# A gated state-space scan with a squared-ReLU FFN on one NeuronCore: units five to twelve put one token on each partition

## The chip, the cores and the metric

The kernel runs on one core of a Trainium2 chip. Its time is the device time of one execution in microseconds (us), given as the median of several runs; smaller is better. A profile is one execution taken by the hardware profiler, with its own span, which is a little shorter than the time of a run.

The engines are named as in the profile: PE is the matrix engine (PEld its weight loads), DVE, ACT and POOL the three elementwise engines, SP the engine that here only issues DMAs. Each engine works its own instructions off in program order. 16 DMA engines move the data.

## What is computed

Four sequences of 768 tokens, eight heads of width 32, a state of 16 x 32 per head. Per head and chunk, with `cum` the running sum of log a:

```
L   = exp(cum[i] - cum[j])  for i >= j, else 0
M   = (C @ B^T) * L                                  # scores, masked
y   = M @ x  +  (C @ state) * exp(cum)               # within the chunk, and from before
state = exp(sum) * state + sum_j B_j x_j exp(cum_last - cum_j)
...
h   = max(y_all_heads @ w_in, 0)                      # 256 -> 2048
out = (h * h) @ w_out                                 # 2048 -> 256
```

The result is a float32 array of 3072 x 256.

## The kernel before

The 3072 tokens are cut into 12 units of 256: unit k is sequence b = k mod 4, third j = k // 4 (`UNITS`). Each unit is two blocks of 128 tokens (i = 0, 1). A token's 256 = 8 x 32 values of y stand on two groups g of 128 partitions (four heads each).

**Token layout.** Each unit's B, C and x are loaded by one DMA each, with two neighbouring tokens on every partition (`ph_load`): partition p holds tokens 2p and 2p + 1, called r = 0, 1. So block i is the partitions 64i to 64i + 63 with both r. A run of the source is two tokens of one head: 128 bytes for B and C, 256 bytes for x, eight runs (heads) to each partition. The output goes out the same way, 2 KB per partition.

**Steps of one unit.** `pc`, `pb` and `px` (POOL) scale C, copy B, and scale x into `jt` and `xs`. `tr` turns `jt` into `bct`: for units 0 to 3 by PE and a copy, from unit 4 on by a DMA transpose that SP issues (`dma_tr`). `ph_mt` makes the scores of the unit from `bct` into PSUM banks 0 to 3; `ph_mask` (DVE, marks `mk`) multiplies them by the causal mask into `mts`. `ph_u` makes the new state's sum from `jt` and `xs`, `ph_carry` the part of y from the state before, `ph_intra` the part within the block. `ph_t` (ACT) copies y into `T`; then eight steps a0 to a7 (`mm1`, letters a to l for units 0 to 11) and A0 to A7 (`mm2`) are the FFN: PE, ACT's relu into `hb`, DVE's square into `h2`, PE again.

**Small products.** They use parts of the 128 x 128 array, four heads q at a time on 32 rows or columns. With two tokens per partition, `ph_mt` needs 16 matmuls (32 rows x 64 columns of weights, 256 columns streamed), `ph_intra` 32 (64 x 32, 128 streamed) and `ph_u` 16 (64 x 32, 64 streamed; 8 where j = 2, since the last state is not needed). `ph_carry` has four full-size ones.

**Order.** The whole program stands in the string `ORDER`: each mark is one step, and each engine's queue gets its instructions in that order. `rg5`, say, is `region(y=4, u=5, mt=5)`: carry of unit 4, `ph_u` of 5, intra of 4, scores of 5, then the copies. In between stand the FFN steps. `ldN` issues the three loads of unit N on SP, `trN` its transpose; the stores of a finished unit are SP's as well. The loads of units 4 to 7 are issued one behind the other early (`ld4 ... ld5 ... tr4 ... ld6 ld7`), those of units 8 to 11 one per region. Before it issues, each DMA waits for the one eight DMAs ahead of it, since the semaphores go round in eight.

Of the kernel before, what the change touches and what calls it, by code (L numbers as in the profile page):

```python
# [11 lines left out]
BF16 = mybir.dt.bfloat16  # L12
AF = mybir.ActivationFunctionType
ALU = mybir.AluOpType
# [16 lines left out]
def kernel(  # L31
# [13 lines left out]
    nc = tc.nc  # L45
    NH, S, D, N = 8, 768, 32, 16
# [8 lines left out]
        qb0 A1 b5 b4 qb1 qb2 qb5 tc2:1:v qb4 tc2:0:a a5 B0 b6 B1 a7 qa5 iv:16:32 px2 a6 mt2 B3 A2 sc2 u2 b7 us2 pb3:a  # L55
# [28 lines left out]

    UNITS = [(b, j) for j in range(3) for b in range(4)]

    eye_f = const.tile([128, 128], FP32, name="eye_f")
    eye_b = const.tile([128, 128], BF16, name="eye_b")
    mask = const.tile([128, 512], BF16, name="mask")
    tri = const.tile([128, 2, 128], BF16, name="tri")  # L90
    warm = const.tile([128, 2], BF16, name="warm")
    quad = const.tile([128, 4], FP32, name="quad")
# [24 lines left out]
    loaded = {}  # L117

    def ph_load(k, what, eng=None, hs=(0, 8)):
        b, j = UNITS[k]  # L120
        src, w = {"B": (B, N), "C": (C, N), "x": (x, D)}[what]
        t = loaded.setdefault(k, {})
        if what not in t:
            t[what] = nat.tile([128, NH, 2 * w], FP32, tag=f"{what}_nat", name=f"{what}_nat{k}")
        (eng or nc.sync).dma_start(
            out=t[what][:, hs[0]:hs[1]],
            in_=_dap(src, ((b * NH + hs[0]) * S + j * 256) * w, [[2 * w, 128], [S * w, hs[1] - hs[0]], [1, 2 * w]]))
# [24 lines left out]
    def prep_c(k, eng, P=None, gs=(0, 1)):  # L152
        b, j = UNITS[k]
        for g in gs:
            p = P_sb if P is None else P
            st = 96 if P is None else 32
            col = (j * 32 if P is None else 0) + b * 8 + 4 * g
            eng.tensor_tensor(  # L158
                out=_fap(jt[k % 3], 128 + 144 * g, [[384, 2], [32, 4], [1, 16]]),
                in0=_fap(loaded[k]["C"], 128 * g, [[16, 2], [32, 4], [1, 16]]),  # L160
                in1=_fap(p, col, [[st, 2], [1, 4], [0, 16]]), op=ALU.mult)

    def prep_b(k, eng, gs=(0, 1)):
        for g in gs:
            o = _fap(jt[k % 3], 16 * g, [[384, 2], [32, 4], [1, 16]])
            i = _fap(loaded[k]["B"], 128 * g, [[16, 2], [32, 4], [1, 16]])
            if eng is nc.scalar:
                eng.copy(out=o, in_=i)
            else:
                eng.tensor_copy(out=o, in_=i)  # L170

    def prep_x(k, eng):
        b, j = UNITS[k]
        xs = prep.tile([128, 2, 256], BF16, tag="xs", name=f"xs{k}")
        n = 2 if k >= 4 else 1
        for r in range(n):
            eng.tensor_tensor(  # L177
                out=_fap(xs, 256 * r, [[256, 2 // n], [32, 8], [1, 32]]),
                in0=_fap(loaded[k]["x"], 32 * r, [[32, 2 // n], [64, 8], [1, 32]]),
                in1=_fap(Pinv, j * 32 + b * 8 + 96 * r, [[96, 2 // n], [1, 8], [0, 32]]), op=ALU.mult)  # L180
        live.setdefault(k, {})["xs"] = xs

# [29 lines left out]
    T = {}  # L212

    def ph_mt(k):
        v = live[k]
        bct = v["bct"]
        for r in range(2):
            for u in range(2):
                for q in range(4):
                    nc.tensor.matmul(  # L220
                        pp[64 * u:64 * u + 64, q, r * 256:r * 256 + 256],
                        bct[32 * q:32 * q + 32, r, 0, u * 64:u * 64 + 64],
                        _fap(bct[32 * q:32 * q + 32], 128 + u * 64, [[128, 2], [384, 2], [1, 64]]),
                        start=True, stop=True, skip_group_check=True,
                        tile_position=(32 * q, 64 * u))
        v["mts"] = big.tile([128, 4, 2, 2, 128], BF16, tag="mts", name=f"mts{k}")

    def ph_mask(k, q):
        nc.vector.tensor_tensor(out=live[k]["mts"][:, q].rearrange("p r g i -> p (r g i)"),  # L229
                                in0=pp[:, q, :], in1=mask, op=ALU.mult)  # L230

    def ph_score(k, q):
        sc = big.tile([128, 512], BF16, tag="sc", name=f"sc{k}_{q}")
# [14 lines left out]
    def ph_carry(k, h, begun):  # L248
        for i in range(2):
            S_i = live[k]["S"][i]  # L250
            if S_i is None:
                continue
            for g in range(2):
                mm(begun, i, range(4), pp[:, h[i], g * 128:(g + 1) * 128], S_i[:, g * 128:(g + 1) * 128],
                   _fap(live[k]["bct"], 128 + g * 128 + i * 64, [[384, 2], [1, 64]]), None)
# [12 lines left out]
    def ph_intra(k, h, begun, qs=range(4)):  # L268
        v = live[k]
        for g in range(2):  # L270
            for r in range(2):
                for i in range(2):
                    for q in qs:
                        hd = 4 * g + q
                        mm(begun, i, [q], pp[32 * q:32 * q + 32, h[i], g * 128:(g + 1) * 128],
                           v["xs"][64 * i:64 * i + 64, r, hd * 32:hd * 32 + 32],
                           v["mts"][64 * i:64 * i + 64, q, r, g, :], (64 * i, 32 * q))

    def ph_t(k, h, engs=None):
        T[k] = tpool.tile([128, 2, 2, 2, 64], BF16, tag="T", name=f"T{k}")  # L280
        if engs is None and h[1] == h[0] + 1:
# [152 lines left out]
    def ph_out(blk):  # L434
        b, j = UNITS[blk]
        osb = opool.tile([128, 512], FP32, tag="osb", name=f"osb{blk}")
        nc.scalar.copy(out=osb, in_=pp[:, 6 if blk == 1 else 7, :])  # L437
        nc.sync.dma_start(out=_dap(out, (b * S + j * 256) * 256, [[512, 128], [1, 512]]), in_=osb)

    def select(t, pattern, base, mult, op=ALU.is_ge):  # L440
# [2 lines left out]
    def prep_p(n, ncol, h):  # L443

        m = n // 2

        def eye_of(n, u):
            return eye_f[0:64, u * 32:u * 32 + 32] if n == 64 else _fap(eye_f, 32 * u, [[64, 2], [1, 32]])

        for r in range(2):  # L450
            for u in range(2):
                nc.tensor.matmul(pp[64 * u:64 * u + 64, h, r * m:(r + 1) * m], _fap(cp[ncol], r, [[2, 64]]),  # L452
                                 eye_of(n, u), start=(r == 0), stop=True, skip_group_check=True,
                                 tile_position=(0, 64 * u))

    with tc.manual_schedule():
# [198 lines left out]
        def one(t):  # L655
# [12 lines left out]
            if name[0] == "q" and len(name) == 2 and name[1] in "abcdefghijkl":  # L668
# [17 lines left out]
                "mb": causal, "pk": picked, "sk": lambda: scan(0), "sp": first_p, "sn": second_scan,  # L686
# [33 lines left out]
        def store(r, eng, c0=0, n=256):  # L720
            t = opool.tile([128, n], FP32, tag="osb", name=f"osl{r}_{c0}")
            eng(out=t, in_=acc(last, r) if n == 256 else pp[:, 1 + c0 // 128, 0:n])  # L722
            (A if c0 else SQ).dma_start(out=_dap(out, (b * S + j * 256) * 256 + r * 256 + c0, [[512, 128], [1, n]]), in_=t)

        for f in range(4, 7):
            mm2(last, f, (0,))
# [37 lines left out]
```

## Time and profile before

| | |
|---|---|
| time, median of 3 runs | 117.67 us (116.44 to 117.77) |
| profiled execution: span | 115.1 us |
| PE busy | 108.9 us, 1623 matmuls |
| DVE, ACT, POOL busy | 84.2, 76.7, 49.8 us |
| moved by DMA | 13.46 MB in 47814 packets |

In the profile a line such as "L220" is the line of the kernel as printed above. In a timeline each row has the start in us from the span's start, the length, the engine (SPq is SP's queue of DMA issues), the line, the operation, what it writes and reads, how many were merged, and in brackets how long the engine stood idle before it and for whom. In the table by windows the columns are the window, its length, the busy time of PE, PEld, DVE, ACT and POOL with the number of instructions, the clock granted to PE, the mean busy share of the 16 DMA engines (over 1 where packets overlap), and GB/s.

### The profile page before, as it was taken

What the parts mean: (1) busy time and instruction counts of PE and PEld (TensorE: products, weight loads), DVE (VectorE), ACT (ScalarE), POOL (GpSimd) and SP (SyncE); (2) the same over time, 40 slices, a digit from 0 to 9 for tenths busy, and PEclk for the clock granted to TensorE, in tenths of its full rate; (3) what the DMA queues carried; (4) which work ended last, traced back from release to release, by engine and by line L of the source; (5) the groups of instructions that cost most, each with busy time, mean ns of one, the idle gap of its engine ahead of it and who ended that gap; (6) DMA issues with size and microseconds to landing.
All of it is one profiled execution on the core that took longest, in us unless ns stands there. A gap on an engine that the chain in (4) does not pass through costs nothing.

```text
span 115.1 us, 3998 instructions
## 1 busy us (share of the span) xinstructions
PE 108.9 (95%) x1623; PEld 93.5 (81%) x1623; DVE 84.2 (73%) x187; ACT 76.7 (67%) x161; POOL 49.8 (43%) x102
## 2 busy tenths in 40 slices
PE   7977969999999999999999999999999999999990
PEld 2344749978898989989989989989989899899980
DVE  2469996779599969969965989849668488445530
ACT  0655667865598756787486686786777776876840
POOL 7369972068599457548602669038020020000000
PEclk9999999999999999999999999999999999999999
DMA  1999999989999913935915926623023020020202
GB/s 29 199 196 145 199 203 189 215 167 210 180 191 211 214 24 108 160 89 155 179 46 122 178 97 123 132 95 73 0 100 68 0 100 0 6 91 0 91 0 91
DMA packets 47814, 13.46 MB, mean 117 GB/s; under 512 B 44276, under 2 KB 45876, under 8 KB 47796
## 3 DMA queue, kind: packets, MB, share of 16 engines
q1 hardware_dynamic: 43828, 10.64, 44.8%
q0 software_dynamic: 1664, 2.10, 10.8%
q10 hardware_dynamic: 2304, 0.48, 2.0%
q8 instruction: 12, 0.20, 0.8%
q14 instruction: 6, 0.05, 0.1%
HBM read 10.58 MB, written 3.15 MB: 119 GB/s over the span
## 4 chain that ended last, share of the span: by engine, by line
PE 87%; DMA 6%; POOL 2%; issue 1%; DVE 1%; ACT 1%; ACTq 0%; DVEq 0%
PE pp L430 36%; PE pp L403 36%; PE pp L245 6%; DMA w_out_b<-in_moe_w_out_dram 6%; PE pp L476 4%; PE pp L220 3%; POOL mts L238 1%; PE pp L195 1%; POOL jt L158 1%; PE pp L452 1%; DVE jt L158 0%; DVE Sd L343 0%; ACT bct L208 0%; PE pp L521 0%; ACT osl L722 0%
## 5 line engine op out<-in xcount | busy, mean ns | idle before, releaser
L408 ACT ACTIVATE hb<-pp 128x512 bf16<-128x512 f32 x96 | 55.0, 599 | 24.7 <-PE pp L403 23.1
L430 PE MATMUL pp<-w_out_b,h 128*128 128x256 bf16 (+1 forms) x400 | 54.3, 268 | 0.8 <-DMA w_out_b<-in_moe_w_out_dram 0.8
L414 DVE TENSOR_TENSOR h<-hb 128x512 bf16<-128x512 bf16 x96 | 45.0, 486 | 12.7 <-ACT hb L408 12.3
L403 PE MATMUL pp<-T,w_in_b 128*128 128x256 bf16 x384 | 54.2, 273 | 0.0
L403 PEld LDWEIGHTS <-w_in_b 128*128 128x128 bf16 x384 | 41.4, 114 | 2.2 <-issue 1.0
L430 PEld LDWEIGHTS <-h 128*128 128x128 bf16 x400 | 37.6, 98 | 5.4 <-DVE T L210 1.1
L229 DVE TENSOR_TENSOR mts<-pp,mask 128x512 bf16<-128x512 f32 x45 | 29.6, 677 | 3.3 <-PE pp L220 3.3
L331 POOL TENSOR_TENSOR Sd<-z,Pquad 128x256 bf16<-128x256 f32 x16 | 11.1, 693 | 32.9 <-DVE z L315 25.7
L177 POOL TENSOR_TENSOR xs<-x_nat,Pinv 128x256 bf16<-128x256 f32 (+1 forms) x19 | 14.4, 776 | 5.2 <-DVE Pinv L546 4.6
L158 POOL TENSOR_TENSOR jt<-C_nat,P_sb 128x128 bf16<-128x128 f32 x22 | 9.4, 449 | 1.5 <-ACT P_sb L688 1.0
L476 PE MATMUL pp<-const-bfloat16-1.0 128*128 128x512 bf16 (+2 forms) x19 | 7.3, 516 | 0.8 <-PEq L748 0.8
L315 DVE SCALAR_TENSOR_TENSOR z<-z,Ptot,us 128x64 f32<-128x64 f32 x8 | 2.2, 281 | 6.3 <-ACT us L299 5.4
L437 ACT COPY osb<-pp 128x512 f32<-128x512 f32 x11 | 6.3, 584 | 0.4 <-PE pp L430 0.4
L245 PE MATMUL pp<-mts,xs 64*32 64x128 bf16 x384 | 5.9, 219 | 0.1
L170 POOL CAST jt<-B_nat 128x128 bf16<-128x128 f32 x17 | 5.4, 341 | 1.4 <-DMA B_nat<-in_B_dram 1.4
L220 PE MATMUL pp<-bct 32*64 32x256 bf16 x192 | 5.1, 279 | 0.9 <-DVE bct L210 0.6
L476 PEld LDWEIGHTS <-const-bfloat16-1.0 128*128 128x128 bf16 x19 | 2.2, 122 | 4.0 <-issue 3.7
L245 PEld LDWEIGHTS <-xs 64*32 64x32 bf16 x384 | 4.2, 90 | 0.6 <-issue 0.4
L282 ACT CAST T<-pp 128x512 bf16<-128x512 f32 x7 | 4.1, 592 | 0.4 <-PE pp L245 0.2
L208 ACT CAST T<-pp 128x256 bf16<-128x256 f32 x8 | 2.6, 375 | 2.6 <-PE pp L245 2.6
L245 PE MATMUL pp<-bct,Sd 128*128 128x128 bf16 x40 | 4.2, 220 | 0.0
L220 PEld LDWEIGHTS <-bct 32*64 32x64 bf16 x192 | 2.1, 102 | 2.0 <-issue 0.6
(62 smaller groups left out, 53.4 us busy)
## 6 DMA issues: line engine op xcount, KB each, us to landing
x_nat<-in_x_dram SPq DMA_DIRECT2D x11, 256.0 KB, 3.7
out_dram<-osb SPq DMA_DIRECT2D x11, 256.0 KB, 3.2
B_nat<-in_B_dram SPq DMA_DIRECT2D x11, 128.0 KB, 3.1
C_nat<-in_C_dram SPq DMA_DIRECT2D x11, 128.0 KB, 3.4
w_in_b<-in_moe_w_in_dram POOLq DMA_DIRECT2D x4, 256.0 KB, 6.8
w_out_b<-in_moe_w_out_dram POOLq DMA_DIRECT2D x4, 256.0 KB, 8.2
x_nat<-in_x_dram ACTq DMA_DIRECT2D x2, 128.0 KB, 3.4
bct<-jt SPq DMA_TRANSPOSE x8, 3.6
```

The lines of the kernel that those rows point to most:

```text
L158: eng.tensor_tensor(out=_fap(jt[k % 3], 128 + 144 * g, [[384, 2], [32, 4], [1, 16]]), in0=_fap(loaded[k]["C"], 128 * g, [[16, 2], [32, 4], ...
L177: eng.tensor_tensor(out=_fap(xs, 256 * r, [[256, 2 // n], [32, 8], [1, 32]]), in0=_fap(loaded[k]["x"], 32 * r, [[32, 2 // n], [64, 8], [1, ...
L220: nc.tensor.matmul(pp[64 * u:64 * u + 64, q, r * 256:r * 256 + 256], bct[32 * q:32 * q + 32, r, 0, u * 64:u * 64 + 64], _fap(bct[32 * q:32 ...
L229: nc.vector.tensor_tensor(out=live[k]["mts"][:, q].rearrange("p r g i -> p (r g i)"), in0=pp[:, q, :], in1=mask, op=ALU.mult)
L245: nc.tensor.matmul(dst, w, v, start=bool(need), stop=False, skip_group_check=True, **({} if pos is None else {"tile_position": pos}))
L331: nc.gpsimd.tensor_tensor(out=_fap(S_d, 0, [[128, 2], [32, 4], [1, 32]]), in0=_fap(z, 0, [[32, 2], [0, 4], [1, 32]]), in1=_fap(Pquad, 4 * ...
L403: nc.tensor.matmul(pp[:, h, i * 256:(i + 1) * 256], _fap(w, g * w.shape[2] + (o // 2) * 512 + 2 * (o % 2) + i, [[4, 128]]), T[blk][:, g].r ...
L408: nc.scalar.activation(out=hb.rearrange("p i t -> p (i t)"), in_=pp[:, h, :], func=AF.Relu)
L414: nc.vector.tensor_tensor(out=h2, in0=hb, in1=hb, op=ALU.mult)
L430: nc.tensor.matmul(dst, h2[:, i, r * 128:(r + 1) * 128], w_out_b[gi][:, 2 * o + i, c0:c1], start=first, stop=(fp == 7 and i == 1), skip_gr ...
L437: nc.scalar.copy(out=osb, in_=pp[:, 6 if blk == 1 else 7, :])
L476: nc.tensor.matmul(pp[:, h, 0:int(cols)], ones_b[:, 0:128], ones_b[:, 0:int(cols)] if dep is None else dep, start=True, stop=True, skip_gr ...
```

## The change

From unit 4 on (`wide(k)`: j > 0) a partition holds one token, and block i is a whole column of 128 partitions:

- each load is issued as two DMAs, one per block, of 128 x 8 runs of one token (64 bytes for B and C, 128 bytes for x); the number of runs per unit doubles, the bytes stay;
- `prep_c`, `prep_b` and `prep_x` read the new places, with the same number of elements and instructions;
- scores: 8 matmuls of 32 x 128 weights with 256 columns in place of 16; intra: 16 of 128 x 32 in place of 32; `ph_u`: 8 (4 where j = 2) in place of 16 (8);
- a second mask `mask_w` for the new order of tokens, made by one POOL instruction (`mw`, a new mark in `ORDER` behind `qb5`);
- `ph_t` writes `T` in the new order, and the store goes out in two pieces of 1 KB per partition;
- the 128-row form of `prep_p`, run once, is one matmul in place of four.

No other mark of `ORDER` moves.

```diff
     def ph_load(k, what, eng=None, hs=(0, 8)):
...
+        if wide(k):
+            for i in range(2):
+                (eng or nc.sync).dma_start(
+                    out=_fap(t[what], i * NH * w, [[w, NH], [1, w]]),
+                    in_=_dap(src, (b * NH * S + j * 256 + i * 128) * w, [[w, 128], [S * w, NH], [1, w]]))
+            return
...
     def ph_mt(k):
...
+        if wide(k):
+            for i in range(2):
+                for q in range(4):
+                    nc.tensor.matmul(pp[:, q, i * 256:i * 256 + 256], bct[32 * q:32 * q + 32, i, 0, :],
+                                     bct[32 * q:32 * q + 32, i, 1:3, :].rearrange("p w t -> p (w t)"),
+                                     start=True, stop=True, skip_group_check=True, tile_position=(32 * q, 0))
+            return
...
     def ph_u(k, h, begun):
...
+        if wide(k):
+            for i in range(2 - last):
+                for q in range(4):
+                    mm(begun, i, [q], pp[32 * q:32 * q + 32, h[i], 256:320],
+                       jt[k % 3][:, i, 0, 32 * q:32 * q + 32],
+                       _fap(v["xs"], i * 256 + q * 32, [[128, 2], [1, 32]]), (0, 32 * q))
+            return
...
     def ph_intra(k, h, begun, qs=range(4)):
...
+        if wide(k):
+            for g in range(2):
+                for i in range(2):
+                    for q in qs:
+                        hd = 4 * g + q
+                        mm(begun, i, [q], pp[32 * q:32 * q + 32, h[i], g * 128:(g + 1) * 128],
+                           v["xs"][:, i, hd * 32:hd * 32 + 32], v["mts"][:, q, i, g, :], (0, 32 * q))
+            return
...
+        def wide_mask():
+            keep_if(mask_w, ones_b, [[0, 4], [1, 128]], 0, -1)
```

On SP, from the last load of unit 3 to the transpose of unit 5, the queue before reads as follows (C_nat4 is the tile that C of unit 4 is loaded into, bct5 the transposed B and C of unit 5, osb0 the finished output of unit 0):

```order
L125 DMA C_nat4_626<-in_C_dram 128x8x32
L125 DMA B_nat4_628<-in_B_dram 128x8x32
L125 DMA x_nat4_630<-in_x_dram 128x8x64
L125 DMA C_nat5_658<-in_C_dram 128x8x32
...
L186 DMA_TRANSPOSE bct4_698<-jt1_110 128x6x128
L125 DMA C_nat6_740<-in_C_dram 128x8x32
...
L125 DMA x_nat7_750<-in_x_dram 128x8x64
L438 DMA out_0_dram<-osb0_807 128x512
L438 DMA out_0_dram<-osb1_814 128x512
L186 DMA_TRANSPOSE bct5_925<-jt2_111 128x6x128
```

and with the change:

```order
L131 DMA C_nat4_625<-in_C_dram 128x8x16 x2
L131 DMA B_nat4_628<-in_B_dram 128x8x16 x2
L131 DMA x_nat4_631<-in_x_dram 128x8x32 x2
L131 DMA C_nat5_660<-in_C_dram 128x8x16 x2
...
L199 DMA_TRANSPOSE bct4_703<-jt1_111 128x6x128
L131 DMA C_nat6_745<-in_C_dram 128x8x16 x2
...
L131 DMA x_nat7_760<-in_x_dram 128x8x32 x2
L487 DMA out_0_dram<-osb0_818 128x512
L487 DMA out_0_dram<-osb1_825 128x512
L199 DMA_TRANSPOSE bct5_920<-jt2_112 128x6x128
```

The order is the same, but 24 loads stand ahead of the transpose of unit 5 where 12 stood, each of as many runs as one had before.

On PE, at the end of region 5, the last product of unit 4 and the first scores of unit 5 stood like this before (the weight load of bct5 waits for the transpose's DMA):

```order
L245 LDWEIGHTS xs4_839
L245 MATMUL pp_120<-mts4_920,xs4_839 32x128
L220 LDWEIGHTS bct5_925
L220 MATMUL pp_120<-bct5_925 64x256
```

and stand now:

```order
L265 LDWEIGHTS xs4_850
L265 MATMUL pp_121<-mts4_907,xs4_850 32x128
L234 LDWEIGHTS bct5_920
L234 MATMUL pp_121<-bct5_920 128x256
```

Eight pairs with bct5 follow one another now, 16 before; the FFN steps stand behind them as they did.

More of the change, by code (lines that the diff above doesn't have):

```diff
@@ L85, with wide @@
     UNITS = [(b, j) for j in range(3) for b in range(4)]
+    def wide(k):
+        return UNITS[k][1] > 0
     eye_f = const.tile([128, 128], FP32, name="eye_f")
@@ L89 @@
     mask = const.tile([128, 512], BF16, name="mask")
+    mask_w = const.tile([128, 512], BF16, name="mask_w")
     tri = const.tile([128, 2, 128], BF16, name="tri")
@@ L165, in prep_b @@
             o = _fap(jt[k % 3], 16 * g, [[384, 2], [32, 4], [1, 16]])
-            i = _fap(loaded[k]["B"], 128 * g, [[16, 2], [32, 4], [1, 16]])
+            i = _fap(loaded[k]["B"], *((64 * g, [[128, 2], [16, 4], [1, 16]]) if wide(k) else
+                                       (128 * g, [[16, 2], [32, 4], [1, 16]])))
             if eng is nc.scalar:
@@ L216, in ph_mt @@
         bct = v["bct"]
+        v["mts"] = big.tile([128, 4, 2, 2, 128], BF16, tag="mts", name=f"mts{k}")
+        if wide(k):
[5 more added lines that the diff above has]
+            return
         for r in range(2):
@@ L225, in ph_mt @@
                         tile_position=(32 * q, 64 * u))
-        v["mts"] = big.tile([128, 4, 2, 2, 128], BF16, tag="mts", name=f"mts{k}")
     def ph_mask(k, q):
         nc.vector.tensor_tensor(out=live[k]["mts"][:, q].rearrange("p r g i -> p (r g i)"),
-                                in0=pp[:, q, :], in1=mask, op=ALU.mult)
+                                in0=pp[:, q, :], in1=mask_w if wide(k) else mask, op=ALU.mult)
     def ph_score(k, q):
@@ L254, in ph_carry @@
                 mm(begun, i, range(4), pp[:, h[i], g * 128:(g + 1) * 128], S_i[:, g * 128:(g + 1) * 128],
+                   live[k]["bct"][:, i, 1 + g, :] if wide(k) else
                    _fap(live[k]["bct"], 128 + g * 128 + i * 64, [[384, 2], [1, 64]]), None)
@@ L280, in ph_t @@
         T[k] = tpool.tile([128, 2, 2, 2, 64], BF16, tag="T", name=f"T{k}")
+        if wide(k):
+            if h[1] == h[0] + 1:
+                nc.scalar.copy(out=_fap(T[k], 0, [[128, 2], [256, 2], [1, 128]]),
+                               in_=_fap(pp, h[0] * 512, [[512, 2], [128, 2], [1, 128]]))
+                return
+            for i in range(2):
+                nc.scalar.copy(out=_fap(T[k], 128 * i, [[256, 2], [1, 128]]),
+                               in_=_fap(pp, h[i] * 512, [[128, 2], [1, 128]]))
+            return
         if engs is None and h[1] == h[0] + 1:
@@ L437, in ph_out @@
         nc.scalar.copy(out=osb, in_=pp[:, 6 if blk == 1 else 7, :])
+        if wide(blk):
+            nc.sync.dma_start(out=_dap(out, (b * S + j * 256) * 256, [[256, 128], [32768, 2], [1, 256]]),
+                              in_=osb.rearrange("p (i d) -> p i d", i=2))
+            return
         nc.sync.dma_start(out=_dap(out, (b * S + j * 256) * 256, [[512, 128], [1, 512]]), in_=osb)
@@ L445, in prep_p @@
         m = n // 2
-        def eye_of(n, u):
-            return eye_f[0:64, u * 32:u * 32 + 32] if n == 64 else _fap(eye_f, 32 * u, [[64, 2], [1, 32]])
+        if n == 128:
+            nc.tensor.matmul(pp[:, h, 0:128], cp[ncol], _fap(eye_f, 0, [[32, 2], [64, 2], [1, 32]]),
+                             start=True, stop=True, skip_group_check=True)
+            return
         for r in range(2):
```

14 lines of the change are left out of this document (8 added, 6 removed).

## The prediction

> **What bounds the kernel now.** I read the page first, for the share of each engine and of the DMA engines.
>
> ```profile
> PE 108.9 (95%) x1623; PEld 93.5 (81%) x1623; DVE 84.2 (73%) x187; ACT 76.7 (67%) x161; POOL 49.8 (43%) x102
> DMA  1999999989999913935915926623023020020202
> q1 hardware_dynamic: 43828, 10.64, 44.8%
> PE 87%; DMA 6%; POOL 2%; issue 1%; DVE 1%; ACT 1%; ACTq 0%; DVEq 0%
> ```
>
> PE is the bound: 95% busy and 87% of the chain that ended last. So what PE saves is saved, and what PE must wait for is lost. The slices of the DMA row (2.9 us each) hold the second fact: from the second to the fourteenth slice, up to 40 us, the DMA engines are full, and after that they have room. The change takes work from PE and gives packets to the DMA queues, so I looked next at the stretch where the two meet, the loads of units 4 to 7, in SP's timeline.
>
> ```profile
> 21.62 2.82 SPq L125 DMA_DIRECT2D C_nat<-in_C_dram  x1
> 24.55 0.52 SPq L125 DMA_DIRECT2D B_nat<-in_B_dram  x1
> 25.16 0.76 SPq L125 DMA_DIRECT2D x_nat<-in_x_dram  x1
> ...
> 27.67 0.86 SPq L125 DMA_DIRECT2D x_nat<-in_x_dram  x1
> 29.07 1.46 SPq L186 DMA_TRANSPOSE bct<-jt  x1
> 30.58 0.56 SPq L125 DMA_DIRECT2D C_nat<-in_C_dram  x1
> ...
> 34.33 0.89 SPq L125 DMA_DIRECT2D x_nat<-in_x_dram  x1
> 35.32 1.00 SPq L438 DMA_DIRECT2D out_dram<-osb  x2
> 36.50 2.11 SPq L186 DMA_TRANSPOSE bct<-jt  x1
> 42.71 0.34 SPq L438 DMA_DIRECT2D out_dram<-osb  x1
> ...
> 45.96 0.58 SPq L125 DMA_DIRECT2D C_nat<-in_C_dram  x1
> 46.59 0.57 SPq L125 DMA_DIRECT2D B_nat<-in_B_dram  x1
> 47.21 0.58 SPq L125 DMA_DIRECT2D x_nat<-in_x_dram  x1
> ```
>
> From 24.55 to 38.6 us SP issues one DMA behind the other: the last eleven loads, the transpose of unit 4 at 29.07, two stores, the transpose of unit 5 at 36.50. The table by windows says when that backlog is gone, and PE's timeline who needs its end.
>
> ```profile
> 24.00:41.50 17.50, 17.39 (x287) 15.21 (x286) 15.87 (x30) 11.78 (x28) 13.24 (x25) 1.00 1.02 185
> 40.50:41.00 0.50, 0.50 (x7) 0.50 (x5) 0.50 (x2) 0.00 (x0) 0.50 (x3) 1.00 0.65 129
> 41.00:41.50 0.50, 0.50 (x7) 0.44 (x6) 0.29 (x1) 0.28 (x1) 0.29 (x1) 1.00 0.00 1
> ```
>
> ```profile
> 35.42 0.42 PE L220 MATMUL pp<-bct 32*64 32x256 bf16 x16
> ...
> 41.90 0.39 PE L245 MATMUL pp<-bct,Sd 128*128 128x128 bf16 x4
> 42.21 0.25 PE L245 MATMUL pp<-xs,jt 64*32 64x64 bf16 x16
> 42.28 0.51 PE L245 MATMUL pp<-mts,xs 64*32 64x128 bf16 x32
> 42.72 0.42 PE L220 MATMUL pp<-bct 32*64 32x256 bf16 x16
> 43.08 0.61 PE L430 MATMUL pp<-w_out_b,h 128*128 128x256 bf16 x4
> ```
>
> The DMA engines have a mean share of 1.02 over the 17.5 us to 41.50 and move nothing from 41.0 on: the transpose of unit 5 has landed by 41.5. PE starts that unit's scores (L220) at 42.72. The slack is 1.2 us, the smallest number of this profile that the change touches.
>
> **The change, part by part.** First the small products. In the rows just shown the region of unit 5 runs from 41.90 to 43.08 by its starts: 0.31 for the carry, 0.07 for `ph_u`, 0.44 for intra, 0.36 for the scores. Per matmul that is 14 ns for intra (32, 128 columns each) and 22 ns for the scores (16, 256 columns): time goes with the columns that each part of the array must stream, not with the count. Eight tiles of 64 x 32 had four streams of 128 columns each in intra; four tiles of 128 x 32 have four each as well. The scores had two rounds of 256 columns on eight tiles and have two on four. Only `ph_u` where j = 2 loses a round. What is left is the stagger of the starts, for which I take 0.06 us per region. The bounds are nothing, and half of the 0.87 us from 42.21 to 43.08, 0.43 us, if all went by the count. Seven regions' worth lie behind the scores of unit 5: 0.4 us gained (0 to 3.0).
>
> Next the loads. Two windows hold packets of one size alone, 0.6 us (35.2 to 35.8) with 128-byte runs and 1.0 us (65.2 to 66.2) with 256-byte runs:
>
> ```profile
> DMA packets 975, 0.12 MB, mean 205 GB/s; under 512 B 975, under 2 KB 975, under 8 KB 975
> DMA packets 906, 0.23 MB, mean 227 GB/s; under 512 B 906, under 2 KB 906, under 8 KB 906
> ```
>
> So 1024 runs, one load, take the engines 0.63 us at 128 bytes and 1.13 us at 256; C, B and x together average 0.80. SP's rows agree: the eleven loads from 24.55 to 35.32 take, without the transpose (29.07 to 30.58) and the 0.54 us before it, 8.72 us, 0.79 each. That stretch goes at the engines' pace. With the change each half has 1024 runs again. The x halves have 128 bytes: 0.63. Runs of 64 bytes are not in the trace; they lie between 0.31 (by bytes) and 0.63 (by runs). But SP's own issue does not go below 0.62 in the quiet rows at 45.96, 46.59 and 47.21. So I take 0.63 for every half, by SP's row for the small ones.
>
> The first half of C of unit 4 leaves SP at 24.5, as the whole did. Then come 23 halves, 14.5 us; the transpose of unit 4, 1.5 (29.07 to 30.58); the two stores, 1.2 (35.32 to 36.50). The transpose of unit 5 is issued at 24.5 + 14.5 + 1.5 + 1.2 = 41.7, where it was 36.5. Its landing takes, by the transposes' own row
>
> ```profile
> DMA to landing us min/median/max: 3.4/3.6/4.1
> ```
>
> 3.4 to 4.1 us, and up to 5.0 for this one (36.50 to 41.5), which had the stores just ahead of it. I take 4.1: it lands at 45.8. PE stands before the scores of unit 5 from 42.7, so it waits 3.1 us. Lower bound: 0.57 per half and 3.4 to land give 43.7, a wait of 1.0. Upper bound: a half costs the 0.79 that a whole load cost in the backlog, and 5.0 to land: 50.4, a wait of 7.7.
>
> The transpose of unit 4 is issued at 24.5 + 11 x 0.63 = 31.4 and lands at 35.0 to 35.5; its scores start at 35.42. At most 0.1 us is lost there, and it is lost inside the later wait. The x of unit 6 comes later too, and POOL's scaling of it stands ahead of the state Sd4 that the carry at 41.90 reads:
>
> ```profile
> 35.23 2.12 POOL L177 TENSOR_TENSOR xs<-x_nat,Pinv 128x256 bf16<-128x256 f32 x3
> 38.78 0.73 POOL L331 TENSOR_TENSOR Sd<-z,Pquad 128x256 bf16<-128x256 f32 x1 [1.42 <-DVE z L315]
> x_nat<-in_x_dram SPq DMA_DIRECT2D x11, 256.0 KB, 3.7
> ```
>
> Its last half is issued at 31.4 + 1.5 + 5 x 0.63 = 36.1, lands 3.7 later at 39.8, two operations of 0.71 and the state's 0.73 end at 41.9. The carry may slip by some tenths; the wait for the scores covers it.
>
> From unit 8 on the loads are spread, those of one unit to a region. A region's length is that from store to store:
>
> ```profile
> 50.94 0.36 SPq L438 DMA_DIRECT2D out_dram<-osb  x1
> 59.29 0.36 SPq L438 DMA_DIRECT2D out_dram<-osb  x1
> ```
>
> In these 8.35 us SP issues six halves, a store and a transpose: 3.8 + 0.4 + 2.1 = 6.3 us, and the loads come a region ahead; nothing is late there. The mask `mw` stands on POOL ahead of this instruction:
>
> ```profile
> 23.32 1.04 POOL L177 TENSOR_TENSOR xs<-x_nat,Pinv 128x512 bf16<-128x512 f32 x1 [4.41 <-DVE Pinv L546]
> L480 POOL TENSOR_SCALAR_AFFINE_SELECT eye_b<-const-bfloat16-1.0 128x128 bf16<-128x128 bf16 x1 | 0.3, 290 | 0.0
> ```
>
> The 4.4 us of idle time hide it: four times the columns of `eye_b` is 1.2 us at most. The masks on DVE, the copies on ACT and the preparations on POOL keep count and size: nothing. The store's 1 KB pieces and `prep_p` (before 16 us, while PE waits for w_out_b) lie beside other work: nothing.
>
> The sum, on the profiled execution: 115.1 + 3.1 - 0.4 = 117.8. The median of the runs is 2.6 above that execution's span, so 120.4.
>
> **The rivals.**
>
> *The queue drains in time.* If small runs cost by their bytes and SP's issue with them, the transpose still lands by 41.5, and only eight regions' stagger is gained: 117.67 - 0.5 = 117.2. Against it stand SP's rows: 0.62 per issue when nothing is queued. Chance 0.15.
>
> *The count pays in full.* 0.43 us for each of eight regions, and no wait: 117.67 - 3.4 = 114.3. The 14 against 22 ns speak against it. Chance 0.05.
>
> *Weight loads come into the open.* Tiles of 128 rows all use the same rows of the array. If their weights cannot be loaded while another tile streams, each round of four pays its load:
>
> ```profile
> L245 PEld LDWEIGHTS <-xs 64*32 64x32 bf16 x384 | 4.2, 90 | 0.6 <-issue 0.4
> 41.19 0.87 PE pp L430 x8
> ```
>
> Five or six rounds of 90 ns per region, 0.5, on seven regions is 3.5 on top: 123.9. Against it: full-size products on the same rows follow one another at 0.109 us (0.87 for 8), with each load hidden. The Trainium skill (TensorE: Matmul & The Clock Gate, on packing small matmuls) says that a weight load overlaps running matmuls only when its row group differs, which by the letter would bring this case; its own step-by-step part also allows the background weight buffer, and the L430 row agrees with that. Chance 0.06.
>
> *PE cools down in the wait.* The kernel's first matmuls, 512 columns each, show a slow start:
>
> ```profile
> 0.85 4.85 PE L476 MATMUL pp<-const-bfloat16-1.0 128*128 128x512 bf16 x11 [0.85 <-PEq L748]
> ```
>
> 0.44 us each is twice the 0.22 that the L430 pace gives for 512 columns, for 4.8 us. If the wait brings that state back, 4 us of work at half pace costs about 2: 122.4. The Trainium skill (the same page, on the clock gate) puts the idle window that throttles at about 3.4 us; no row here shows one. The wait of 3.1 is just below; it decides from there on. Chance 0.12.
>
> **How the numbers follow.** The forecast, a wait of about 3 us, has 0.62; its own range is 118.8 to 122.5, from waits of 1.5 to 5.2. About 2% either way, 115.3 to 120.0, is what a measurement of this kernel can tell from no change. The forecast lies above 120.0 in some 6 of 10 of its cases: 0.37, plus 0.06 and 0.12, is 0.55 for slower. Faster is half of the full count's chance, 0.03; the rest, 0.42, is no change. The range 117.2 to 123.5 leaves about one in ten out on each side.
>
> **What would show it.** In the profile of the changed kernel: a PE wait of 2 to 4 us on the DMA that writes bct, at about 43 us and once only; SP's issue of the second transpose at 41 to 42 us in place of 36.5; queue q1 with some 25,000 packets more at the same bytes; and regions behind it shorter by less than 0.15 us. I am wrong if that transpose lands before 43 (no wait), if the regions shrink by 0.3 or more, or if they grow.

## The result, and the profile after

| | before | after |
|---|---|---|
| time, median | 117.4 us of 4 runs (116.44 to 117.77) | 124.97 us of 4 runs (124.23 to 126.38) |
| ratio, 95% interval | | 1.0647 [1.0558, 1.0736] |
| profiled execution: span | 115.1 us | 123.3 us |
| PE busy | 108.9 us, 1623 matmuls | 110.7 us, 1375 matmuls |

The kernel is slower by 6.5%. (Medians below are of all runs of a kernel; the ratios leave disturbed runs out on both sides, so the two can differ by more than a per cent, and split_issue, with one undisturbed run in four (118.92 us), has no ratio.)

The page of the changed kernel, the rows that answer to those shown of before:

```profile
PE 110.7 (90%) x1375; PEld 93.3 (76%) x1377; DVE 84.6 (69%) x187; ACT 77.0 (62%) x161; POOL 50.0 (41%) x103
DMA  1999999948899899878487786699505020020112
q1 hardware_dynamic: 69684, 10.64, 54.5%
PE 65%; DMA 13%; SPq 6%; DVE 5%; ACT 4%; POOL 3%; issue 1%; POOLq 0%; DVEq 0%; ACTq 0%
```

The chain that ended last was PE's for 87%; it is now PE's for 65%, with 13% for transfers and 6% for SP's issues. Queue q1 moves the same 10.64 MB in 69684 packets in place of 43828. The DMA engines (slices of 3.1 us) are now at seven tenths or more in most slices up to the twenty-eighth, 86 us, where before they had room from 40 us on.

SP's timeline, with two issues merged in each row of a load:

```profile
17.47 9.08 SPq L131 DMA_DIRECT2D C_nat<-in_C_dram  x2
26.66 1.38 SPq L131 DMA_DIRECT2D B_nat<-in_B_dram  x2
...
33.07 1.80 SPq L131 DMA_DIRECT2D x_nat<-in_x_dram  x2
34.98 1.32 SPq L199 DMA_TRANSPOSE bct<-jt  x1
36.35 2.04 SPq L131 DMA_DIRECT2D C_nat<-in_C_dram  x2
...
44.87 1.80 SPq L131 DMA_DIRECT2D x_nat<-in_x_dram  x2
46.76 1.00 SPq L487 DMA_DIRECT2D out_dram<-osb  x2
47.94 1.25 SPq L199 DMA_TRANSPOSE bct<-jt  x1
```

The transpose of unit 4 leaves SP at 34.98 (before 29.07), that of unit 5 at 47.94 (before 36.50). The 22 half-loads from 26.66 on take 20.01 us up to the end at 46.67, less 1.37 for the transpose: 18.64, or 0.85 each.

PE's timeline shows who waits for the two (L265 is carry, `ph_u` and intra, L234 the scores):

```profile
35.40 0.42 PE L265 MATMUL pp<-mts,xs 64*32 64x128 bf16 x32
40.56 0.61 PE L234 MATMUL pp<-bct 32*128 32x256 bf16 x8 [4.75 <-DMA bct<-jt]
41.11 1.03 PE L475 MATMUL pp<-w_out_b,h 128*128 128x256 bf16 x4
41.93 3.49 PE L448 MATMUL pp<-T,w_in_b 128*128 128x256 bf16 x16
...
49.58 0.40 PE L265 MATMUL pp<-mts,xs 128*32 128x128 bf16 x16
51.56 0.40 PE L234 MATMUL pp<-bct 32*128 32x256 bf16 x8 [1.59 <-DMA bct<-jt]
...
58.89 0.39 PE L265 MATMUL pp<-bct,Sd 128*128 128x128 bf16 x4
59.20 0.24 PE L265 MATMUL pp<-xs,jt 128*32 128x64 bf16 x8
59.27 0.40 PE L265 MATMUL pp<-mts,xs 128*32 128x128 bf16 x16
59.60 0.40 PE L234 MATMUL pp<-bct 32*128 32x256 bf16 x8
59.93 2.06 PE L448 MATMUL pp<-T,w_in_b 128*128 128x256 bf16 x16
```

There are two waits: 4.75 us ahead of the scores of unit 4 and 1.59 ahead of those of unit 5, which start at 51.56, 8.84 later than before (42.72). Behind that point 0.64 us is won back (8.84 less the 8.2 that the span grew). The products are shorter: from the start of the carry to the end of the scores it is now 58.89 to 59.93, 1.04, where it was 1.18 (41.90 to 43.08). Intra took 0.44 and takes 0.33.

The row at 41.93 has another reading: 16 matmuls in 3.49 us, twice as long as the pace of 0.109 each allows. The table by windows gives the granted clock, in the column ahead of the DMA share:

```profile
38.00:40.00 2.00, 0.00 (x0) 0.00 (x0) 0.00 (x0) 0.00 (x0) 0.62 (x1) 0.58 0.82 91
40.00:42.00 2.00, 1.44 (x13) 0.77 (x14) 0.73 (x2) 0.00 (x0) 0.00 (x0) 0.50 0.81 83
42.00:44.00 2.00, 2.00 (x11) 1.40 (x10) 1.24 (x3) 0.72 (x2) 0.45 (x1) 0.50 1.01 141
44.00:46.00 2.00, 2.00 (x15) 1.56 (x14) 1.94 (x5) 1.62 (x3) 1.22 (x3) 0.71 0.94 89
46.00:48.00 2.00, 2.00 (x21) 1.82 (x20) 1.42 (x4) 0.66 (x2) 1.84 (x4) 1.00 0.84 119
```

PE's clock is halved inside the first wait and stays so until 45 us.

### The profile page after: what moved, and what is told of

Same layout as the page of the kernel before. It is cut to its first block, busy times and chain, and to the rows that moved or that the text cites. A ratio compares the mean times of both kernels' runs of the same rounds, so it can differ in the third digit from the quotient of the medians.

```text
span 123.3 us, 3539 instructions
## 1 busy us (share of the span) xinstructions
PE 110.7 (90%) x1375; PEld 93.3 (76%) x1377; DVE 84.6 (69%) x187; ACT 77.0 (62%) x161; POOL 50.0 (41%) x103
## 3 DMA queue, kind: packets, MB, share of 16 engines
q1 hardware_dynamic: 69684, 10.64, 54.5%
## 4 chain that ended last, share of the span: by engine, by line
PE 65%; DMA 13%; SPq 6%; DVE 5%; ACT 4%; POOL 3%; issue 1%; POOLq 0%; DVEq 0%; ACTq 0%
PE pp L448 27%; PE pp L475 27%; DMA bct<-jt 7%; SPq L131 5%; PE pp L265 5%; DVE h L459 4%; DMA x_nat<-in_x_dram 3%; DMA a_nat<-in_a_dram 3%; PE pp L234 2%; ACT hb L453 1%; PE pp L526 1%; PE pp L208 1%; PE pp L241 1%; POOL Sd L376 1%; POOL xs L189 1%
## 5 line engine op out<-in xcount | busy, mean ns | idle before, releaser
L448 PE MATMUL pp<-T,w_in_b 128*128 128x256 bf16 x384 | 55.8, 279 | 0.0
L249 DVE TENSOR_TENSOR mts<-pp,mask_w 128x512 bf16<-128x512 f32 x32 | 21.4, 680 | 7.9 <-PE pp L234 7.9
L168 POOL TENSOR_TENSOR jt<-C_nat,P_sb 128x128 bf16<-128x128 f32 x22 | 10.1, 478 | 2.0 <-DMA C_nat<-in_C_dram 1.0
L249 DVE TENSOR_TENSOR mts<-pp,mask 128x512 bf16<-128x512 f32 x13 | 8.3, 685 | 1.8 <-PE pp L241 1.8
L234 PE MATMUL pp<-bct 32*128 32x256 bf16 x64 | 3.4, 289 | 6.3 <-DMA bct<-jt 6.3
L234 PEld LDWEIGHTS <-bct 32*128 32x128 bf16 x64 | 1.0, 94 | 7.3 <-DMA bct<-jt 6.7
L182 POOL CAST jt<-B_nat 128x128 bf16<-128x128 f32 x17 | 4.7, 303 | 2.6 <-DVE a_cl L518 1.4
L265 PE MATMUL pp<-mts,xs 64*32 64x128 bf16 (+1 forms) x256 | 5.3, 229 | 0.0
L265 PE MATMUL pp<-bct,Sd 128*128 128x128 bf16 x40 | 4.3, 223 | 0.0
L265 PEld LDWEIGHTS <-xs 64*32 64x32 bf16 (+1 forms) x256 | 3.3, 98 | 0.7 <-issue 0.5
L221 ACT COPY bct<-pp 128x384 bf16<-128x384 bf16 (+1 forms) x6 | 2.6, 452 | 1.8 <-PE pp L208 1.8
```

Source lines behind the costliest of these rows:

```text
L168: eng.tensor_tensor(out=_fap(jt[k % 3], 128 + 144 * g, [[384, 2], [32, 4], [1, 16]]), in0=_fap(loaded[k]["C"], *((64 * g, [[128, 2], [16, ...
L234: nc.tensor.matmul(pp[:, q, i * 256:i * 256 + 256], bct[32 * q:32 * q + 32, i, 0, :], bct[32 * q:32 * q + 32, i, 1:3, :].rearrange("p w t ...
L265: nc.tensor.matmul(dst, w, v, start=bool(need), stop=False, skip_group_check=True, **({} if pos is None else {"tile_position": pos}))
L448: nc.tensor.matmul(pp[:, h, i * 256:(i + 1) * 256], _fap(w, g * w.shape[2] + (o // 2) * 512 + 2 * (o % 2) + i, [[4, 128]]), T[blk][:, g].r ...
```

## The experiments

The profile leaves four questions: whether products or loads make the loss; whether it is the number of runs, of issues, or of packets; whether it is their place in SP's queue; and what the halved clock costs. Eleven kernels went to the chip, each beside runs of the kernel before on the same chip (medians 116.63, 117.16 and 117.63 us in the three groups).

**The loads alone: half_runs.** The kernel before, with its own products, and the loads as two DMAs:

```diff
+        if k >= 4:
+            for r in range(2):
+                (eng or nc.sync).dma_start(
+                    out=t[what][:, :, r * w:(r + 1) * w],
+                    in_=_dap(src, (b * NH * S + j * 256 + r) * w, [[2 * w, 128], [S * w, NH], [1, w]]))
+            return
```

> The kernel before, with each load of units 4 to 11 issued as two DMAs, one for each of a partition's two tokens: the runs of the changed kernel (64 and 128 bytes, twice as many) with the products of the kernel before. Theory (runs and issues of the loads make the whole loss): waits on bct before the scores of units 4 and 5 of 4 to 5 and 1 to 3 us, 124.5 to 126 us, a little over the changed kernel, since the products' gain of some 0.6 us is missing. Rival (the products or their tiles lose something too): clearly below the changed kernel, 118 to 123.

Measured: 125.55 us (123.09 to 126.59), ratio 1.063 [1.0524, 1.0735], the whole loss of the change. PE's timeline of this kernel (L226 is its scores):

```profile
44.60 0.51 PE L251 MATMUL pp<-mts,xs 64*32 64x128 bf16 x32
50.48 0.65 PE L226 MATMUL pp<-bct 32*64 32x256 bf16 x16 [5.37 <-DMA bct<-jt]
```

The same wait, on the transpose of unit 5, with products of the old shape. The wait that was expected at unit 4 did not come: PE reached those scores at 37.74, 2.3 us later than before.

**The products alone: products_only.** The changed kernel without the branch for `wide(k)` in `ph_load`: the loads are those of before, so that tokens inside units 4 to 11 are taken in another order.

> The changed kernel with the loads of the kernel before (one DMA each, two tokens per run): the 24 extra issues and the extra runs are gone, everything else of the change stays. What is left out: the tokens of units 4 to 11 lie in the wrong order, so the output is not the reference's. Theory (the products gain 0.06 to 0.1 us a region and lose nothing): no wait on bct, 116.5 to 117.2 us. Rival (half the count pays by the count): 114. Rival (weight loads come into the open): over 118.

Measured: 116.9 us (114.7 to 118.68, 12 runs), ratio 0.9946 [0.9897, 0.9995]; span 113.9, no wait on `bct`. The products are worth about half a per cent, 0.6 us, and bring no stall. Loads and products are thus apart: the loads lose 6.3%, the products gain 0.5%.

**Issues or runs: split_issue.** The kernel before, each load from unit 4 on issued as two DMAs of four heads. The runs are those of before (44212 packets in q1, where before has 43828); only the issues double.

```diff
-        (eng or nc.sync).dma_start(
-            out=t[what][:, hs[0]:hs[1]],
+        for hs in ((0, 4), (4, 8)) if k >= 4 else (hs,):
+            (eng or nc.sync).dma_start(
+                out=t[what][:, hs[0]:hs[1]],
```

> The kernel before, with each load of units 4 to 11 issued as two DMAs of four heads each: as many runs and bytes as before (128 and 256 bytes), twice as many issues. Theory (the number of runs sets the pace of the queue): the DMA engines need 0.80 us per load as before, two issues of 512 runs some 0.9, so the transpose of unit 5 lands at most 1.5 us later against a slack of 1.2: 117.4 to 118 us, no wait over 0.5 us on bct. Rival (the number of issues sets it): the transposes are as late as in the changed kernel, 34.98 and 47.94 us, and the time is 124 to 125.

Measured: 122.2 us (118.92 to 123.82, 4 runs). Both sides of this expectation were missed: the time lies between them. Without a single run of the source more it is 5.6 us above before in the median, and 2.3 at its lowest; split_warm below, with the same loads, gives a steadier figure. SP's timeline, PE's and the windows of the profiled execution (123.82 us):

```profile
25.72 0.99 SPq L126 DMA_DIRECT2D B_nat<-in_B_dram  x2
...
40.81 1.05 SPq L126 DMA_DIRECT2D x_nat<-in_x_dram  x2
41.96 0.92 SPq L439 DMA_DIRECT2D out_dram<-osb  x2
43.06 1.25 SPq L187 DMA_TRANSPOSE bct<-jt  x1
```

```profile
47.57 0.65 PE L221 MATMUL pp<-bct 32*64 32x256 bf16 x16 [4.16 <-DMA bct<-jt]
48.16 1.03 PE L431 MATMUL pp<-w_out_b,h 128*128 128x256 bf16 x4
```

```profile
25.70:42.00 16.30, 16.30 (x278) 14.38 (x272) 14.42 (x29) 10.92 (x26) 10.45 (x21) 1.00 0.73 128
```

From 25.72 to 41.86, less the transpose of 1.37, 22 halves take 14.77 us: 0.67 each, at a DMA share of 0.73. Eight of the eleven pairs took 0.99 to 1.06, those of C and B like those of x with twice the bytes, while a whole load of 1024 runs took 0.79 in the backlog: in these pairs SP's issue sets the pace, not the engines. The transpose of unit 5 leaves at 43.06. With the runs of the change on top the halves take 0.85 and it leaves at 47.94. Of the 11.4 us over before (36.50), some 6.6 thus come with the number of issues, and in these two profiles 4.9 are left for the runs that each of them has. The second part is not firm. In half_runs, move_5 and warm_after (the last two are described below) as many halves with as many runs stand ahead of this transpose, and it leaves earlier, with 0.82, 0.73 and 0.79 us for each half:

```profile
46.10 2.35 SPq L192 DMA_TRANSPOSE bct<-jt  x1
45.92 1.24 SPq L199 DMA_TRANSPOSE bct<-jt  x1
44.46 1.24 SPq L199 DMA_TRANSPOSE bct<-jt  x1
```

So the number of issues makes the larger part, and the runs 1.4 to 4.9 us. That each DMA waits for the one eight ahead does not set the pace: in the changed kernel the halves issued from 24 to 48 us land 3.0 to 3.6 us after their issue (medians of B, x and C), and eight issues at 0.85 take 6.8.

These are the packets of a stretch in the backlog, first of before, then of after:

```profile
DMA packets 12493, 2.15 MB, mean 187 GB/s; under 512 B 12489, under 2 KB 12489, under 8 KB 12489
```

```profile
DMA packets 9726, 0.80 MB, mean 95 GB/s; under 512 B 9724, under 2 KB 9724, under 8 KB 9724
```

Before, 24.5 to 36.0 us: 1086 packets per us. After, 26.6 to 35.0: 1158 per us, at half the bytes, with this DMA share (0.83) in the windows' row of the same stretch:

```profile
26.60:35.00 8.40, 8.40 (x136) 7.27 (x135) 6.76 (x13) 6.00 (x17) 5.47 (x10) 1.00 0.83 95
```

Over such a stretch the queue moves about as many packets per us with runs half as long, and a half-load has as many as a whole one had. The size of a packet still counts: with the shares of the two stretches (1.06 of 16 engines before, 0.83 after) a packet keeps an engine busy for 15.6 ns before and for 11.5 ns after. Nor are the engines full after. What holds the halves at 0.73 to 0.85 us, where the shortest pairs take 0.57 to 0.60 for each, no run here separates.

**The place in the queue: move_5 and move_67.** The changed kernel with one mark of `ORDER` moved, `ld5` behind `tr4`:

```diff
-A3 ld5 pb4 ina2 inb2 tr4 ca2
+A3 pb4 ina2 inb2 tr4 ld5 ca2
```

> The changed kernel with unit 5's six half-loads alone moved behind unit 4's transpose. As many DMAs stand ahead of unit 5's transpose as in the changed kernel. If the sum of all that is ahead of it sets the end, unit 4's transpose is issued 4 to 5 us earlier (28 to 31 us) and its scores do not wait, but unit 5's transpose stays at 44 to 48 us, one PE wait of 4 to 9 us stands before unit 5's scores, and the time stays at 122 to 125.5. If the first wait and what follows it make the loss, the time falls to 119 to 120.

and with the loads of units 6 and 7 moved, those of unit 5 left (and `px6` behind `pb6`, since POOL would else stand before x of unit 6):

```diff
-qb7 ld6 ld7 mt3
+qb7 mt3
...
-rg4 tr5 C0
+rg4 tr5 ld6 C0
...
-tr6 mk5
+tr6 ld7 mk5
```

> The changed kernel with the half-loads of units 6 and 7 alone moved (behind the transposes of units 5 and 6); unit 5's stay ahead of unit 4's transpose. Unit 4's transpose is issued at 32 to 35 us as in the changed kernel. If what stands ahead of it makes the first wait, 1 to 4.5 us of wait remain at unit 4's scores and the time is 118.5 to 122.5 (the upper end with a halved clock behind the wait). If the loads behind it held up its landing (5.5 us in the changed kernel), it now lands within 3.6 us, the wait is under 2 us and the time 117 to 118.5. Unit 5's scores do not wait in either case.

Measured for move_5: 126.69 us (125.71 to 127.22), ratio 1.0868 [1.0755, 1.0981]. PE's timeline:

```profile
35.75 0.40 PE L234 MATMUL pp<-bct 32*128 32x256 bf16 x8
...
44.00 0.28 PE L265 MATMUL pp<-bct,Sd 128*128 128x128 bf16 x2 [1.52 <-POOL Sd L376]
...
49.61 0.61 PE L234 MATMUL pp<-bct 32*128 32x256 bf16 x8 [4.93 <-DMA bct<-jt]
50.16 1.03 PE L475 MATMUL pp<-w_out_b,h 128*128 128x256 bf16 x4
50.98 1.06 PE L448 MATMUL pp<-T,w_in_b 128*128 128x256 bf16 x4
```

The transpose of unit 4, issued at 29.50, is in time and the first wait is gone. Nothing is won by it: the transpose of unit 5 still leaves SP at 45.92, and PE waits 4.93 us there instead. The 1.52 us on the state `Sd` is the late x of unit 6, which the late queue also brings. Rows of four matmuls take 1.03 to 1.06 in place of 0.60: the halved clock now falls where no second wait hides it, and the time is 1.7 us above that of the change.

Measured for move_67: 119.95 us (117.65 to 124.74), ratio 1.0174 [0.999, 1.0359]. PE's timeline of its profiled run (117.65 us):

```profile
36.66 0.40 PE L234 MATMUL pp<-bct 32*128 32x256 bf16 x8 [1.80 <-DMA bct<-jt]
...
43.83 0.40 PE L234 MATMUL pp<-bct 32*128 32x256 bf16 x8
```

The transpose of unit 4 leaves at 33.01, lands in 3.6 us, and PE waits 1.80 us for it, as the second theory has it; unit 5 does not wait. But in move_5 that transpose landed in 3.0 us with loads behind it, so these do not hold it up by themselves. The median lies in the range of the first theory, and the four runs are too far apart to price what is left. In three of them more than half of the loss is gone; the fourth, 124.74 us, has no profile. As far as these runs tell, the twelve halves of units 6 and 7 make the large part, those of unit 5 the rest.

**The place, all of it: respread_after, respread2_after, respread2_before, wide_last.** respread_after makes both moves above; respread2_after also moves `ld8` behind `tr7`, `ld9` behind `tr8` and `px8` behind `pb8`; respread2_before does the same to the kernel before; wide_last puts one token on a partition for units 8 to 11 alone (`UNITS[k][1] > 1`, with the columns of `prep_p` put in the order that this mixture needs).

> The changed kernel with four marks of the order moved: ld5 behind tr4, ld6 behind tr5, ld7 behind tr6, px6 behind pb6, so that only 6 halves stand ahead of the transpose of unit 4 and 12 ahead of that of unit 5. Theory (the place in the queue is the loss, not the total of the runs): transposes issued at about 31 and 38 us, no wait over 1 us on bct, 116.5 to 117.8 us. Rival (short runs make every transfer late): a wait of 3 us or more stays, over 120.

> The changed kernel with every load moved behind the DMA transpose that it stood ahead of: units 5 to 9 (the run before moved 5 to 7 and kept one wait of 1.7 us, at unit 7's scores). If the loss is only the place in SP's queue, no PE wait on bct over 0.5 us is left, tr7 is issued some 4 us earlier (at about 52 us), and the time shows the products' gain: 116.0 to 116.6, a ratio of 0.99 to 0.997. If small runs cost more than their place (more DMA time beside everything else), it stays at 117.5 to 118.5, or a new wait of 1 us or more appears at unit 8 or on POOL's x.

> Control: the kernel before with the loads of units 5 to 9 moved behind the transposes, as in the run of the changed kernel that came out equal to before. If the move itself costs nothing, it is the same as before, 0.995 to 1.005, and the full-height products are then worth nothing that can be measured once the loads are halves. If the move costs 0.5 to 1% (POOL waits for its loads later), the products' gain of 0.5% is what paid for it.

> One token per partition for units 8 to 11 alone; the loads of units 4 to 7 are those of the kernel before. If the loss comes from the 24 half-loads in the backlog up to 40 us, nothing of it is left: no PE wait on bct, 116.2 to 116.8, a ratio of 0.99 to 1.0. If small runs cost wherever they stand, half of the loss stays: 120 to 121.

| kernel | median, us (range, runs) | ratio, 95% interval |
|---|---|---|
| respread_after | 117.79 (115.36 to 120.81, 12) | 0.9981 [0.9921, 1.004] |
| respread2_after | 117.89 (116.01 to 119.35, 12) | 1.0037 [0.9977, 1.0097] |
| respread2_before | 116.75 (115.46 to 118.25, 13) | 0.9975 [0.9922, 1.0028] |
| wide_last | 117.06 (116.39 to 119.5, 12) | 1.0043 [1.0, 1.0087] |

All four are equal to the kernel before to within 1%, wide_last 0.3 us above the range that was expected for it. With the loads behind the transposes the 6.5% are gone, at the same packets and the same issues; wide_last, with the old loads in the backlog, never has them. The place of the loads in SP's queue is the cause. PE's rows of respread_after and of respread2_after, the only waits for `bct` in each:

```profile
60.53 0.40 PE L234 MATMUL pp<-bct 32*128 32x256 bf16 x8 [1.70 <-DMA bct<-jt]
```

```profile
75.38 0.40 PE L234 MATMUL pp<-bct 32*128 32x256 bf16 x8 [0.75 <-DMA bct<-jt]
```

The wait of 1.70 us at unit 7 went with the second move (its transpose left at 53.30 in place of 56.13), but 0.75 us appeared at unit 9, and the time did not fall to the 116.0 to 116.6 that the theory expected. So the half per cent of products_only could not be had with the loads as halves. Where it goes was not settled: the profile of respread2_after (span 114.8) has a lower clock, 0.66, from 8 to 12 us, which that of products_only (113.9) has not, and this alone may be as large. Nothing here beats the kernel before by more than its interval.

**The clock: split_warm and warm_after.** 14 or 16 matmuls of 512 columns on constants stand ahead of the region in which PE waits: in split_issue ahead of `rg5`, in the changed kernel ahead of `rg4`.

```diff
-sa4 rg5
+sa4 id14:512 rg5
```

```diff
-c2 rg4 tr5
+c2 id16:512 rg4 tr5
```

> The kernel with the loads from unit 4 on split by heads (same runs; 122.2 before), with 14 idle matmuls of 512 columns (about 3.0 us) ahead of the region in which PE waits 4.2 us. They fill the wait and move nothing else: transpose 5 lands at the same time, about 47.5. If the wait itself halves the clock and that costs about 2.2 us more, the rows behind it run at 1.00 and the time falls to 119.5 to 120.5. If the halved clock costs nothing or comes from something else, it stays at 121.5 to 122.5 with the clock at 0.5 behind 45 us.

> The changed kernel with 16 idle matmuls of 512 columns (about 3.5 us) ahead of the region with its first wait (4.75 us, unit 4's scores). The clock should then stay at 1.00 behind 38 us. If unit 5's scores wait for the transpose alone, which SP issues at 47.9 whatever PE does, the time stays at 124 to 125.5 and the second wait grows by what the first stretch saves. If the halved clock behind the first wait sets the end, it falls by 2 to 3 us to about 122.5.

Measured for split_warm: 120.99 us (120.95 to 121.22), ratio 1.0392 [1.0325, 1.046], span 119.2, half a microsecond above the expected range. PE's timeline:

```profile
42.27 3.22 PE L477 MATMUL pp<-const-bfloat16-1.0 128*128 128x512 bf16 x13
...
46.84 0.42 PE L221 MATMUL pp<-bct 32*64 32x256 bf16 x16 [0.62 <-DMA bct<-jt]
47.20 0.61 PE L431 MATMUL pp<-w_out_b,h 128*128 128x256 bf16 x4
```

(Of the 14 idle matmuls 13 are on record.) The wait shrinks to 0.62 us, the clock stays at 1.00 and four matmuls behind it take 0.61 where split_issue needed 1.03. The scores start 0.73 us earlier than in split_issue (46.84 against 47.57), and the span is 2.9 shorter: between these two profiles 2.2 us is the price of the halved clock. The medians differ by 1.2 only, with the runs of split_issue 5 us apart. With the clock kept up, the doubled issues alone cost 3.9%.

Measured for warm_after: 123.45 us (122.3 to 126.1), ratio 1.0567 [1.0471, 1.0662], below the range of the first theory and not far enough for the second.

```profile
48.04 0.40 PE L234 MATMUL pp<-bct 32*128 32x256 bf16 x8 [2.42 <-DMA bct<-jt]
48.37 1.00 PE L475 MATMUL pp<-w_out_b,h 128*128 128x256 bf16 x4
```

As the first theory has it, the scores of unit 5 still wait for the transpose, now 2.42 us in place of 1.59. That transpose left SP at 44.46 and not at 47.94, because B of unit 4 had left at 24.43 in place of 26.66, ahead of anything that was added; and the clock was halved behind this wait. The run confirms which wait ends last; the profiled times it does not compare cleanly.

**The sum over the runs.** Two terms give each profiled execution: how late the scores of unit 5 start (against 42.72), and what a halved clock costs behind them. (The profiled executions of half_runs and split_issue, 126.59 and 123.82 us, lie above their medians.)

| kernel | scores of unit 5 | late by | span | longer by (115.1) | difference | half clock behind |
|---|---|---|---|---|---|---|
| after | 51.56 | 8.84 | 123.3 | 8.2 | -0.6 | no (it lay ahead) |
| split_warm | 46.84 | 4.12 | 119.2 | 4.1 | 0.0 | no |
| split_issue | 47.57 | 4.85 | 122.1 | 7.0 | 2.1 | yes |
| half_runs | 50.48 | 7.76 | 124.9 | 9.8 | 2.0 | yes |
| warm_after | 48.04 | 5.32 | 121.4 | 6.3 | 1.0 | yes |
| move_5 | 49.61 | 6.89 | 124.6 | 9.5 | 2.6 | yes |

The two kernels without a half clock behind the scores end as late as the scores start, less the products' 0.6 in after. The others pay for the clock: 2.0 and 2.1 us with the old products; with the new ones, adding the 0.6 that these win, 1.6 in warm_after and 3.2 in move_5.

## Why the prediction was right in its sign and wrong in its size

**Right:** the mechanism and its place. The half-loads of units 4 to 7 push the transpose of unit 5 back in SP's queue, PE waits for it, and this is the whole loss (half_runs, move_5, respread_after). The products gain little and lose nothing (products_only); the mask, 0.81 us on POOL at 20.08, is hidden. From unit 8 on PE does not wait for a transpose in the changed kernel.

**The step that failed: "So I take 0.63 for every half, by SP's row for the small ones."** The halves took 0.85 in the profile of the change. On 22 of them that is 4.8 us. The quiet rows at 46 us do not show what an issue costs in the backlog. The price was at hand in the rows of before: 0.79 us for a whole load of 1024 runs in that very stretch, which I kept as the upper bound ("a half costs the 0.79 that a whole load cost in the backlog"). The runs show that this was the value to take: halves of 1024 runs took 0.73 to 0.85 in four profiles, and halves of 512 runs still 0.67. The landing that this bound gave, 50.4, was passed as well. The rest is the start: B of unit 4 leaves SP at 26.66, where 24.5 + 0.63 = 25.1 was forecast. That start moves from run to run (25.10 in move_5, 24.43 in warm_after). The landing was half a microsecond shorter than taken, 3.57 against 4.1. Together: 45.8 + 4.8 + 1.5 - 0.1 (the transpose and stores ahead) - 0.5 = 51.5, the measured landing. From there the sum holds: the wait's end is 5.7 later than forecast and the products give 0.64 in place of 0.4 (0.14 in the region of unit 6 and 0.09 in the later ones of 1.11 us, where 0.06 was taken), so that 117.8 becomes 123.3, the measured span. Only the step from span to median, taken as 2.6, was 1.7 (124.97 less 123.3), which takes 0.9 off again.

The Trainium skill (DMA: Bandwidth & Descriptors, section Measured) gives a floor of about 10.5 ns for a packet, for loads that GpSimd (POOL) issues; taken as the price on one of 16 engines, which the page does not say, a half-load of 1024 packets is, as an estimate, 0.67 us. The backlog is dearer: 1158 packets per us at a share of 0.83 of 16 engines is 11.5 ns each, and the engines are not full all the time.

**"At most 0.1 us is lost there"**, at the scores of unit 4, failed as well: 4.75 us. Its transpose left 3.6 later than the 31.4 forecast, by the same two errors, and took 5.5 us to land (34.98 to 40.5, where PE goes on). Why it took that long stays open: in move_5, with loads behind it in the same queue too, it took 3.0, and in move_67, with stores behind it, 3.6. But the first wait sets nothing. Without it PE would have come to the scores of unit 5 earlier by the 4.75 us and by some 2.1 that the halved clock took, and would have waited there 8.4 us instead of 1.59, for the same landing: move_5 takes the first wait away and is no faster.

**The rivals.** *The queue drains in time* fell at once. *The count pays in full* fell: at most 0.14 us per region, not 0.43. *Weight loads come into the open* fell: 16 full-height products of intra take 0.33 us, less than 32 half-height ones took, and by the letter of the rule of the Trainium skill (TensorE: Matmul & The Clock Gate, on packing small matmuls: a weight load overlaps only where the row group differs) they should have been slower; the measurement decides. *PE cools down in the wait* happened, with about the price that was worked out, "about 2" us: 2.2 between the profiles of split_issue and split_warm. In the changed kernel's profile it came behind the first wait and was covered by the second, so it added nothing to the time; it does in every kernel with one long wait.

## What to carry to other kernels

Price an added DMA by a whole row of its kind in the stretch where it will stand, by its runs and not by its bytes alone: here half the bytes in as many runs took SP's queue 0.85 us against 0.79, and half the runs still 0.67. Then read what stands behind it in the issuing queue: a load that is needed a region later belongs behind the transpose that is needed now, and moving it was worth the whole 6.5% here. And where several waits follow one another, only the one that ends last is worth anything; removing the first made the kernel slower.

## What the runs showed that was not expected

- An issue of 512 runs costs SP at least 0.5 us and one of 1024 runs 0.57 (the shortest pairs took 0.99 and, in move_5, 1.15). Halving a DMA therefore adds some 0.4 us of issue, even where runs and bytes stay.
- Waits of PE of 1.59, 1.70 and 1.80 us left the clock at 1.00; waits of 2.42 (warm_after), 4.16, 4.75, 4.93 and 5.37 us were followed by a halved one. The wait of 2.42 is shorter than the idle window of about 3.4 us that the Trainium skill states (TensorE: Matmul & The Clock Gate, on the clock gate); PE was busy for 1.61 us from 44 to 48, the stretch around it.
- In some executions the clock is halved early too, as in after from about 8 to 14 us, where PE waits often but never over a microsecond:

```profile
8.00:12.00 4.00, 3.10 (x56) 1.64 (x57) 3.27 (x9) 2.13 (x7) 2.72 (x5) 0.50 1.10 178
```

The profiles of half_runs, split_issue, move_5 and respread2_before have it, those of before, products_only, split_warm and move_67 do not. What decides it stays open.
